# Loading the first weight block of a gated mixer from two DMA queues

## The chip, the core and the metric

The kernel runs on one core of a Trainium2 chip. The metric is the device time in microseconds (us) of one execution; the time before is the median of three runs. The profile comes from one further, profiled execution.

## The reference

The inputs are bfloat16: x is 2048 x 1024. Two branches are computed from the same x and blended per row.

```python
x = A_x
g = _sigmoid((x * gate_w).sum(-1, keepdims=True))
a = _A_ref(x, A_wqkv, A_wo)                 # 32 heads, window of 8 keys at distance 2, softmax, output projection
b = _B_ref(x, B_w_in, B_w_sp, B_b_sp, B_w_out)
return g * a + (1 - g) * b

def _B_ref(x, w_in, w_sp, b_sp, w_out):     # F = 3584, Fh = 1792
    z = _gelu(jnp.einsum('bsd,df->bsf', x, w_in))
    z1 = z[..., :Fh].copy()
    z2 = _layernorm(z[..., Fh:], axis=-1)
    g = jnp.einsum('ts,bsf->btf', w_sp, z2) + b_sp[None, :, None]
    return jnp.einsum('bsf,fd->bsd', z1 * g, w_out)
```

The part that this case is about is the very first product: x times the columns of w_in that give z2.

## The kernel before

Nearly all of SBUF that the kernel uses is one tile, `arena`, cut into regions by hand. `xT` holds x transposed (eight k tiles of 128 rows, 2048 columns). `w2` holds the z2 half of w_in, also as eight k tiles. The instruction order on every engine is the order of the program text (`manual_schedule`); semaphores are added by the framework, and a DMA that reuses a semaphore waits for that semaphore's earlier transfer.

The stages, all paced by TensorE: a warm-up on constants (L91, `warm_up`); the transposes of the first two row tiles (L246) and the `quad`, which is row tiles 0 and 1 times two 512-column blocks of `w2` (both in `z2_quad`); `z2_tile(i, 0)` for row tiles 2 to 15 (L231); q, k and v (L446); the rest of z2 (L231 again); z1 (L482); the spatial product (L496); the output projections and the blend (L509, L519, L527). The attention itself runs on VectorE beside the matmuls, placed by a planner that counts TensorE columns (`Beat`); none of its steps lie in the first 40 us.

What the start consists of:

- SP's queue, in order: row tiles 0 and 1 of x as plain loads into `xn` (L404, 256 KB each); the eight k tiles of w_in's first 1024 z2 columns into `w2` (L406, 256 KB each, 128 rows of 2 KB); then row tiles 2 to 15 of x as transposing loads straight into `xT` (L411), with the first q, k and v weights in between.
- TensorE: seven warm-up matmuls, then 16 transposes of `xn` (L246) into PSUM tiles `pt`.
- VectorE (L250) and ScalarE (L252) each copy half of every `pt` into `xT`: VectorE the k tiles 0, 1 and 4, 5, ScalarE the k tiles 2, 3 and 6, 7, in the order row tile 0 then row tile 1.
- TensorE then runs the quad, k tile by k tile:

```python
for kt in range(KT):
    for i in range(2):
        for c in range(2):
            z2_mm(quad[i][c], i, c, kt, ZW[c])      # L231
```

Each k tile of `w2` is thus read by four matmuls before the next one is needed. After the quad, ScalarE evicts it with Gelu (L236), for which it loads another table first. `z2_tile(2, 0)` is the first to need a row tile that came by a transposing load.

Of the kernel before, what the change touches and what calls it, by code (L numbers as in the profile page):

```python
# [25 lines left out]
FH = 1792  # L26
NF = FH // P
ZC = 512
# [23 lines left out]
def kernel(  # L52
# [13 lines left out]
    nc = tc.nc  # L66
# [10 lines left out]
    def reg(off, n):  # L77
        return arena[:, off:off + n]
# [7 lines left out]
    ones = nc.const_aps.tensor(1.0, [P, 512], BF)  # L86
# [48 lines left out]
    w2 = reg(CD_OFF, KT * W2P).rearrange("p (k c) -> p k c", k=KT)  # L135
# [18 lines left out]
    win_v = B_w_in.rearrange("(k p) c -> p k c", p=P)  # L154
    wsp_v = B_w_sp.rearrange("(a t) s -> a t s", t=P)
    wo_v = A_wo.rearrange("(g h d) n -> g h d n", g=NG, h=HG, d=DH)
    sync = nc.sync
# [244 lines left out]

    for i in range(2):
        sync.dma_start(xn[:, i, :], x_v[:, i, :])  # L404
    for kt in range(KT):
        sync.dma_start(w2[:, kt, 0:2 * ZC], win_v[:, kt, FH:FH + 2 * ZC])  # L406
    for i in range(2, 16):
        if i == 14:
            load_w(0, 2)
# [190 lines left out]
```

## Time and profile before

| | |
|---|---|
| median of 3 runs | 716.31 us (715.63 to 717.37) |
| profiled execution | 715.24 us |
| its span, first to last instruction | 713.5 us |
| TensorE busy | 709.5 us, 99% of the span |
| VectorE, ScalarE, GpSimd busy | 413.7, 246.3, 14.0 us |
| DMA queues with transfers of the kernel | one (q1), 92.36 MB |
| SP's issues L404 / L406 / first L411 | from 0.74 / 1.65 / 5.64 us |
| ScalarE's first table load / first copy L252 | 0.73 / 4.39 us |
| first matmul L231 | 5.67 us |

Times inside the profile count from the first instruction. "SPq" marks an instruction in SP's queue, which issues a DMA; the transfer's landing is given separately, as the time from issue until the last byte is confirmed. "x8" is the number of merged instructions, and a bracket gives the idle time ahead of the first one and what ended it. A matmul is pipelined, so its listed duration is longer than the distance to the next one.

### The profile page before, as it was taken

What the parts mean: (1) busy time and instruction counts of PE and PEld (TensorE: products, weight loads), DVE (VectorE), ACT (ScalarE), POOL (GpSimd) and SP (SyncE); (2) the same over time, 40 slices, a digit from 0 to 9 for tenths busy, and PEclk for the clock granted to TensorE, in tenths of its full rate; (3) what the DMA queues carried; (4) which work ended last, traced back from release to release, by engine and by line L of the source; (5) the groups of instructions that cost most, each with busy time, mean ns of one, the idle gap of its engine ahead of it and who ended that gap; (6) DMA issues with size and microseconds to landing.
All of it is one profiled execution on the core that took longest, in us unless ns stands there. A gap on an engine that the chain in (4) does not pass through costs nothing.

```text
span 713.5 us, 8376 instructions
## 1 busy us (share of the span) xinstructions
PE 709.5 (99%) x3373; PEld 365.1 (51%) x3373; DVE 413.7 (58%) x428; ACT 246.3 (35%) x451; POOL 14.0 (2%) x23
## 2 busy tenths in 40 slices
PE   9999999999999999999999999999999999999998
PEld 4466666666655554444444444444444444444444
DVE  0000589999999999999999999511222112221111
ACT  4434544435379885253331221111111111121111
POOL 1000000000000211000000000000000000000000
PEclk9999999999999999999999999999999999999999
DMA  8974984785673035974449770592400213002210
GB/s 238 191 179 104 255 201 100 202 197 164 176 200 125 0 115 114 208 262 144 173 152 277 275 174 2 184 180 64 132 1 0 54 49 119 1 1 59 60 45 30
DMA packets 176759, 92.89 MB, mean 130 GB/s; under 512 B 145232, under 2 KB 166992, under 8 KB 176208
## 3 DMA queue, kind: packets, MB, share of 16 engines
q1 hardware_dynamic: 176720, 92.36, 48.7%
q8 instruction: 26, 0.43, 0.3%
q14 instruction: 13, 0.11, 0.1%
HBM read 47.71 MB, written 28.38 MB: 107 GB/s over the span
## 4 chain that ended last, share of the span: by engine, by line
PE 99%; DVE 0%; issue 0%; DVEq 0%
PE ps L496 27%; PE ps L446 23%; PE ps L231 14%; PE psb L519 14%; PE ps L482 14%; PE psa L509 8%; PE pw L91 0%; PE pt L246 0%; DVE arena L527 0%; DVE arena L250 0%; DVEq L527 0%
## 5 line engine op out<-in xcount | busy, mean ns | idle before, releaser
L496 PE MATMUL ps<-arena 128*128 128x512 bf16 x896 | 193.9, 379 | 0.0
L446 PE MATMUL ps<-arena 128*128 128x512 bf16 x768 | 165.9, 379 | 0.0
L496 PEld LDWEIGHTS <-arena 128*128 128x128 bf16 x896 | 87.7, 98 | 105.7
L446 PEld LDWEIGHTS <-arena 128*128 128x128 bf16 x768 | 110.7, 144 | 55.1
L519 PE MATMUL psb<-arena 128*128 128x512 bf16 (+2 forms) x462 | 101.6, 373 | 0.0
L274 DVE TENSOR_TENSOR arena<-arena 128x8192 bf16<-128x8192 bf16 x16 | 70.8, 4423 | 51.8 <-DMA arena<-k_d 51.6
L231 PE MATMUL ps<-arena 128*128 128x512 bf16 (+1 forms) x512 | 97.3, 352 | 0.4 <-DVE arena L250 0.4
L527 DVE SCALAR_TENSOR_TENSOR arena<-psb,omg,arena 128x512 bf16<-128x512 f32 (+2 forms) x33 | 24.3, 735 | 125.3 <-PE psb L519 109.3
L482 PE MATMUL ps<-arena 128*128 128x512 bf16 x448 | 96.9, 379 | 0.0
L500 ACT CAST arena<-ps 128x512 bf16<-128x512 f32 x56 | 32.8, 586 | 162.4 <-PE ps L496 135.7
L449 ACT CAST arena<-ps 128x512 bf16<-128x512 f32 x96 | 55.7, 585 | 92.8 <-PE ps L446 88.2
L277 DVE TENSOR_TENSOR arena<-arena 128x4096 bf16<-128x4096 bf16 (+1 forms) x64 | 77.5, 1210 | 1.9
L231 PEld LDWEIGHTS <-arena 128*128 128x128 bf16 x512 | 50.1, 98 | 47.3 <-issue 0.5
L519 PEld LDWEIGHTS <-arena 128*128 128x128 bf16 x462 | 44.7, 98 | 52.1
L307 DVE TENSOR_TENSOR arena<-arena,att_A 128x8192 bf16<-128x8192 bf16 x16 | 70.7, 4422 | 0.2
L482 PEld LDWEIGHTS <-arena 128*128 128x128 bf16 x448 | 43.9, 98 | 52.6
L501 DVE TENSOR_TENSOR arena<-arena 128x512 bf16<-128x512 bf16 x56 | 23.6, 422 | 72.3 <-ACT arena L500 72.3
L526 ACT ACTIVATE arena<-psa,g_s 128x512 f32<-128x512 f32 (+2 forms) x33 | 22.2, 674 | 122.9 <-PE psa L509 109.7
L509 PE MATMUL psa<-arena 128*128 128x512 bf16 (+2 forms) x264 | 60.0, 373 | 0.0
L484 ACT ACTIVATE arena<-ps 128x512 bf16<-128x512 f32 x56 | 32.2, 597 | 52.4 <-PE ps L482 39.4
L236 ACT ACTIVATE arena<-ps 128x512 bf16<-128x512 f32 (+1 forms) x64 | 34.3, 538 | 24.4 <-PE ps L231 24.3
L509 PEld LDWEIGHTS <-arena 128*128 128x128 bf16 x264 | 25.6, 98 | 30.0
(53 smaller groups left out, 258.4 us busy)
## 6 DMA issues: line engine op xcount, KB each, us to landing
arena<-k_d SPq DMA_DIRECT2D x8, 960.0 KB, 7.5
arena<-v_d SPq DMA_DIRECT2D x8, 960.0 KB, 5.1
z_d<-arena SPq DMA_DIRECT2D x14, 512.0 KB, 3.7
arena<-z_d SPq DMA_DIRECT2D x4, 1792.0 KB, 7.1
arena<-in_A_wqkv_dram SPq DMA_DIRECT2D x24, 256.0 KB, 4.6
arena<-in_B_w_in_dram SPq DMA_DIRECT2D x4, 1024.0 KB, 6.6
q_d<-arena SPq DMA_DIRECT2D x32, 128.0 KB, 2.3
k_d<-arena SPq DMA_DIRECT2D x32, 128.0 KB, 2.3
```

What stands on the lines that cost most here:

```text
L231: nc.tensor.matmul(ps[:, 0:N], xT[:, kt, i * P:(i + 1) * P], w2[:, kt, ZC * c:ZC * c + N], start=(kt == 0), stop=(kt == KT - 1))
L236: nc.scalar.activation(z2[:, i, ZC * c:ZC * c + n], ps[:, 0:n], ACT.Gelu_apprx_tanh, accum_out=s1[:, 4 * i + c:4 * i + c + 1])
L274: TT(prod.rearrange("p (w j c) -> p w j c", w=W, j=8, c=C), in0, in1, ALU.mult)
L277: return lambda: TT(pv[:, :, 0:half], pv[:, :, 0:half], pv[:, :, half:2 * half], ALU.add)
L307: TT(prod.rearrange("p (w j d h) -> p w j d h", w=W, j=8, d=DH, h=HG), in0, in1, ALU.mult)
L446: nc.tensor.matmul(ps[:].rearrange("p (t c) -> p t c", t=4), lhsT, wgt[:, :, kt, :], start=(kt == 0), stop=(kt == KT - 1))
L449: nc.scalar.copy(st[:, j % 4, :], ps[:])
L482: nc.tensor.matmul(ps[:], w1[:, kt, (f % 4) * P:(f % 4 + 1) * P], xT[:, kt, 512 * c:512 * (c + 1)], start=(kt == 0), stop=(kt == KT - 1))
L496: nc.tensor.matmul(ps[:], z2[:, i, f * P:(f + 1) * P], wsp[:, i, :, :].rearrange("p a t -> p (a t)"), start=(i == 0), stop=(i == 15))
L500: nc.scalar.copy(gsb, ps[:])
L509: nc.tensor.matmul(psa[:, 0:nw], oT_slots[a % 3][:, kt, :], wo_sb[:, kt, n0:n0 + nw], start=(kt == 0), stop=(kt == KT - 1))
L519: nc.tensor.matmul(psb[:, 0:nw], z1c[:, f, aa * P:(aa + 1) * P], w_out_sb[:, f, n0:n0 + nw], start=(f == 0), stop=(f == NF - 1))
```

## The change

ScalarE first copies 16 columns of the constant ones into the place where k tile 0 of `w2` is going to land. K tiles 0, 2, 4 and 6 are then loaded by DMAs that ScalarE issues, and k tiles 1, 3, 5 and 7 by SP, behind x's two row tiles as before. The load of k tile 0 overwrites the 16 columns, so it waits for the copy, and the three loads behind it on ScalarE wait with it.

```diff
     for i in range(2):
         sync.dma_start(xn[:, i, :], x_v[:, i, :])
+    nc.scalar.copy(w2[:, 0, 0:16], ones[:, 0:16])
     for kt in range(KT):
-        sync.dma_start(w2[:, kt, 0:2 * ZC], win_v[:, kt, FH:FH + 2 * ZC])
+        queue = sync if kt % 2 else nc.scalar
+        queue.dma_start(w2[:, kt, 0:2 * ZC], win_v[:, kt, FH:FH + 2 * ZC])
     for i in range(2, 16):
```

In the changed program the order on ScalarE is: table load, the new copy, the loads of k tiles 0, 2, 4 and 6, the four copies L252, the Gelu table load. The fourth of these loads waits for x's row tile 1, whose semaphore it reuses. On SP it is: row tiles 0 and 1, k tiles 1, 3, 5 and 7, row tile 2 and so on; row tile 2 waits for k tile 1, whose semaphore it reuses (before: k tile 0's). On TensorE nothing is added, removed or reordered.

## The prediction

> **What bounds the kernel now.** I read the page's first part, then the chain of waits over the first 13 us, the timeline of the same stretch, and last the DMA view in windows narrow enough to hold one transfer each.
>
> ```profile
> PE 709.5 (99%) x3373; PEld 365.1 (51%) x3373; DVE 413.7 (58%) x428; ACT 246.3 (35%) x451; POOL 14.0 (2%) x23
> ```
>
> TensorE is busy for 709.5 of 713.5 us. Whatever happens to loads in the first 15 us is therefore worth what it moves TensorE's stream by, and no more. The chain shows where that stream is not closed:
>
> ```profile
> 0.77 2.82 PE pw L91 x7
> 3.60 1.71 PE pt L246 x16
> 5.31 0.02 issue
> 5.33 0.30 DVE arena L250
> 5.64 0.03 issue
> 5.67 7.50 PE ps L231 x34
> ```
>
> Warm-up matmuls and the 16 transposes run until 5.31, and the first real matmul (L231, k tile 0 of the quad) starts at 5.67: a gap of 0.36 us. The chain names the VectorE copy L250, which is the fourth one, as the releaser. That copy writes k tiles 4 and 5 of row tile 1, which the first matmul does not read. The DMA view gives the transfer that it does read:
>
> ```profile
> arena<-in_A_x_dram SPq DMA_DIRECT2D x1, 256.0 KB, 2.4
> ...
> arena<-in_B_w_in_dram SPq DMA_DIRECT2D x1, 256.0 KB, 4.0
> ...
> arena<-in_B_w_in_dram SPq DMA_DIRECT2D x1, 256.0 KB, 4.2
> ...
> arena<-in_B_w_in_dram SPq DMA_DIRECT2D x1, 256.0 KB, 4.4
> ...
> arena<-in_A_x_dram SPq DMA_TRANSPOSE x1, 5.8
> ```
>
> These are x's row tile 0 (issued at 0.74), then k tiles 0, 1 and 2 of w_in (issued at 1.65, 2.12 and 2.60), then row tile 2 (issued at 5.64). The last column is the time from issue to landing. So k tile 0 lands at 1.65 + 4.0 = 5.65, which is what the first matmul waited for; k tile 1 at 6.32, k tile 2 at 7.00. The same view gives 7.57, 8.24, 9.12, 9.80 and 10.41 for k tiles 3 to 7, and 4.09 for row tile 1. The timeline has the queues:
>
> ```profile
> 0.73 1.28 ACT L252 ACT_TABLE_LOAD   x1 [0.73 <-PEq L584]
> 0.74 0.87 SPq L404 DMA_DIRECT2D arena<-in_A_x_dram  x2
> ...
> 1.65 3.89 SPq L406 DMA_DIRECT2D arena<-in_B_w_in_dram  x8
> ...
> 4.39 1.65 ACT L252 COPY arena<-pt 128x256 bf16<-128x256 bf16 x4 [2.37 <-DVE arena L250]
> ...
> 5.64 8.78 SPq L411 DMA_TRANSPOSE arena<-in_A_x_dram  x5
> 5.67 8.58 PE L231 MATMUL ps<-arena 128*128 128x512 bf16 x39 [0.37 <-DVE arena L250]
> ```
>
> SP issues a transfer every 0.47 us, but k tiles land 0.57 to 0.88 us apart: the transfers, not the issues, set the pace (the DMA engines' share is 0.97 and more from 3.6 us on). L231 matmuls follow each other every 0.217 us (112 in 24.33 us by the chain over 30 us), so the quad reads a new k tile every 0.87 us and finishes in 6.94 us. Each later k tile has more to spare than the one before: k tile 1 is needed at 6.54, k tile 7 at 11.76. Only k tile 0 is late.
>
> **The change, part by part.** *The hold.* ScalarE now copies 128x16 values first. Its table load stays at 0.73 and ends at 2.01. A copy can follow a table load directly:
>
> ```profile
> 203.36 1.28 ACT L236 ACT_TABLE_LOAD   x1
> 204.66 0.60 ACT L236 ACTIVATE arena<-ps 128x512 bf16<-128x512 f32 x1
> ```
>
> A 128x16 instruction of ScalarE takes 0.21 us (L387, 208 ns), and the step from a finished copy to what waits for it is about 0.03 us (L250's first copy ends at 4.35, L252 starts at 4.39). So k tile 0 is issued at 2.01 + 0.01 + 0.21 + 0.04 = 2.27 instead of 1.65, 0.62 us later. ScalarE has nothing else until 4.39, so the copy itself costs nothing; without that idle time it would cost its 0.21.
>
> *Where k tile 0 lands.* No transfer in this trace comes from ScalarE's queue, so I bound it. From below: with nothing ahead of it, as for row tile 0, it lands 2.4 us after issue, at 4.67, earlier than now. From above: if the DMA engines serve it only after all four odd tiles, it takes k tile 4's present landing, 8.24. Between these: SP's queue goes from x straight to k tile 1, issued at 1.65 and next to move when x is through. K tiles 0 and 1 are then in flight together, and 512 KB take as long side by side as in turn. Both end where the second ends today, at 6.32. I take 6.32, because it needs only that bytes move at the rate the landings show and that two queues share them evenly.
>
> *The first matmul.* Now its weight load is done (4.995 to 5.14) before k tile 0 lands, and only the matmul waits, 0.02 us. In the changed program the weight load carries the wait for k tile 0, so it follows the landing; L246's loads and their matmuls start 0.11 us apart. First matmul: 6.32 + 0.02 + 0.11 = 6.45, against 5.67: **+0.78 us**. Bounds: below, 5.21, when the third L250 copy ends that the quad's third matmul reads (-0.46); above, 8.24 + 0.13 = 8.37 (+2.70).
>
> *The other k tiles.* All eight still move the same 2 MB. With a start at 6.45, k tile 1 is needed at 7.32, 2 at 8.19, 7 at 12.5; even if each pair lands with its later member, the landings above are 7.57 for 2 and 3, 9.12 for 4 and 5, 10.41 for 6 and 7. Cost 0. If this cover were gone, each late tile would cost its lateness.
>
> *ScalarE's queue.* Four issues at 0.47 us (SP's price) from 2.27, the last also waiting for row tile 1's landing (4.09) by the reuse of its semaphore: done by about 4.6. Behind them stand the four L252 copies, which start at 4.39 now: 0.2 us later. Their first reader is k tile 2's weight load, at 7.18 now and 7.96 then. At twice the price per issue the copies would still have started by 6.1, and the third, which row tile 1's weights need at 8.4, would end by 7.4. Cost 0 either way. Behind the copies the Gelu table load (6.05) has until 12.12.
>
> *SP's queue.* Four issues fewer, so SP is free at 3.65 instead of 5.54. But row tile 2 reuses a semaphore: now it waits for k tile 0 (issued 5.64, the landing was 5.65), in the changed program for k tile 1. At 6.32 + 0.03 + 5.8 it lands at 12.15; the quad's end, where it is needed, moves to 6.45 + 6.94 = 13.39. Cost 0, gain 0: row tiles landing sooner release nothing, since no L231 wait behind the quad shows in the waits of TensorE from 12 to 200 us.
>
> *The sum.* 0.78 us, all of it ahead of a stream that is closed to its end. The profiled execution is 715.24 (span 713.5 and 1.7 around it): 716.02. The three timed runs have a median of 716.31, 1.07 above the profiled one, from 715.63 to 717.37. On the median: **717.1 us**. Of this kernel a measurement tells about 0.2%, 1.43 us, from no change; the forecast lies within it.
>
> **Rivals.**
>
> *K tile 0 keeps its place (no change, or a little gain).* If an engine turns to the other queue after each whole transfer, then with x's last rows running when k tile 0 arrives, k tile 0 is next, ahead of k tile 1, and lands near 5.65 as now: +0.11, 716.4. In a run where no slow engine holds it up, it could land nearer 5.1, and the bound is -0.46: 715.85. For it: in the DMA view data begin to move about 1.0 us after the first issue, so at 2.27 + 1.0 k tile 0 would meet x's tail, which lands at 4.09. Against: nothing here shows turns. The Trainium skill's DMA: Bandwidth & Descriptors (Queues, rings and completion order) says that each engine goes round its queues and drains a packet of some 9 to 17 descriptors from one before it turns to the next, about one of these transfers' share on an engine; by that rule the time would be this rival's. The trace has one queue only and cannot show it.
>
> *K tile 0 stands behind the odd tiles (slower).* SP's are issued at 1.65, 2.12, 2.60 and 3.07, with two ahead of 2.27. If engines take work in order of issue, k tile 0 is third and lands at k tile 2's 7.00: first matmul at 7.13, +1.46, 717.8. If they empty SP's queue first, it is fifth: +2.70, 719.0. The point that decides is a landing past 6.97. For it: the DMA engines are full from 3.6 us on, and a k tile lands 4.0 to 5.3 us after its issue where row tile 0 took 2.4, so there is a line to stand in. Against: a queue of its own need not wait behind another's.
>
> *TensorE's clock falls back in the longer gap (slower).* The warm-up's weight loads are 0.43 us apart, L231's 0.217: half speed until some 5.2, 4.4 us after the first matmul. The gap in TensorE grows from 0.36 to 1.14 us. If that were enough to lose full speed and it took 4.4 us to regain, 2.2 us of work would be lost on top: +2.98, 719.3. Against: the 0.36 us gap did no harm. The Trainium skill's TensorE: Matmul & The Clock Gate (What's actually happening) has the clock fall only after an idle window of about 3.4 us; by that rule 1.14 us cost no speed, and the trace agrees as far as its 0.36 us go.
>
> **How the numbers follow.** Forecast (+0.78) 0.42; place kept 0.15; behind the odd tiles 0.27; clock 0.11; something that gains over 1.43 us 0.05, for which I see no mechanism: the whole gap is 0.36 us and the copies allow 0.46. Within 0.2%: 0.42 + 0.15 = 0.57. Slower: 0.27 + 0.11 = 0.38. Faster: 0.05. The range runs from the gain's bound, 715.85, less 0.4 for the scatter of a median of such runs, to the clock rival: 715.4 to 719.3. For the likeliest case alone: 716.3 to 717.9.
>
> **What would show it.** In the changed profile: ScalarE's copy near 2.0 and its four DMA issues from 2.27; the first L231 matmul near 6.45, released by w_in's transfer; then L231 closed at 0.217 us spacing, and the end as much later as the first matmul. A start at or before 5.8 means place kept; past 7.1, behind the odd tiles; a start near 6.45 with spacing 0.43 after it, the clock. A gap in L231 behind the quad would mean that row tiles or ScalarE's copies became late, which I put at nothing.

## Result: 0.5% slower; in the trace, half of it a late first tile, half of it a slow clock

The changed kernel takes 719.58 us (median of 7 runs, 717.23 to 720.83), the kernel before 715.80 (7 runs, 715.52 to 717.37) beside it: ratio 1.0047, 95% interval 1.003 to 1.0063. A second comparison (last experiment) gave 1.006 (1.0045 to 1.0075). The profiled execution has a span of 716.9 us against 713.5, so 3.4 us are to be found. (The medians differ by 3.8; the traces account for the profiled executions.)

The page of the changed kernel: busy times, the two DMA queues, the chain by engine.

```profile
PE 711.3 (99%) x3373; PEld 365.3 (51%) x3373; DVE 413.7 (58%) x428; ACT 246.7 (34%) x452; POOL 14.0 (2%) x23
...
q1 hardware_dynamic: 176144, 91.31, 48.2%
q10 hardware_dynamic: 576, 1.05, 0.4%
...
PE 99%; DMA 1%; ACT 0%; DVE 0%; issue 0%; DVEq 0%
```

TensorE has the same 3373 matmuls and is busy 1.8 us longer: some of its work ran slower. And 1% of the chain is now a DMA. The chain over the first 13 us says where:

```profile
0.73 1.28 ACT L405
2.01 0.01 issue
2.02 0.21 ACT arena L405
2.24 0.02 issue
2.26 4.99 DMA arena<-in_B_w_in_dram
7.25 0.14 issue
7.38 5.73 PE ps L231 x18
```

The hold is as costed: table load, copy, issue at 2.26. But k tile 0 lands at 7.25, and the first L231 matmul starts at 7.38 instead of 5.67: 1.71 us. The other half stands in the windows of the same profile (columns: stretch, its length, busy time of PE, PEld, DVE, ACT and POOL, granted clock, DMA share, GB/s):

```profile
5.20:7.30 2.10, 0.18 (x3) 0.00 (x0) 0.45 (x2) 2.03 (x4) 0.00 (x0) 1.00 1.01 348
7.40:8.59 1.19, 1.19 (x6) 0.56 (x7) 0.00 (x0) 0.02 (x1) 0.00 (x0) 1.00 1.04 382
8.60:12.00 3.40, 3.40 (x10) 1.21 (x8) 0.00 (x0) 0.00 (x0) 0.00 (x0) 0.50 1.19 258
12.01:15.40 3.39, 3.39 (x17) 1.54 (x16) 0.00 (x0) 0.00 (x0) 0.00 (x0) 1.00 0.87 197
```

TensorE does nothing for 2 us, works 1.2 us at full speed, and then has half its clock for 3.41 us (8.59 to 12.01): 8 weight loads where the next stretch has 16. At 0.427 us per matmul instead of 0.216 that stretch loses 3.41 x 0.495 = 1.69 us. 1.71 + 1.69 = 3.40, the whole difference.

Where k tile 0 spent its 5 us, by the DMA view. First the time to landing of SP's k tile 1 (issued 1.64), SP's k tile 3 (2.12) and ScalarE's k tile 0 (2.26); then what the queues moved in 2.0 to 4.2 us, and in 4.6 to 6.4 (q1 is SP's queue, q10 ScalarE's; packets, MB, share of the 16 engines):

```profile
arena<-in_B_w_in_dram SPq DMA_DIRECT2D x1, 256.0 KB, 5.3
...
arena<-in_B_w_in_dram SPq DMA_DIRECT2D x1, 256.0 KB, 6.1
...
arena<-in_B_w_in_dram ACTq DMA_DIRECT2D x1, 256.0 KB, 5.0
...
q1 hardware_dynamic: 363, 0.67, 85.0%
...
q1 hardware_dynamic: 182, 0.34, 54.8%
q10 hardware_dynamic: 126, 0.24, 41.8%
```

Until past 4.2 only SP's queue moves: x, then k tile 1. ScalarE's queue moves its first data at 4.45, 2.2 us after the issue, and from then on both move, 0.34 and 0.24 MB in the 1.8 us shown. Three tiles are in flight at once, and all three land late: 6.9, 7.25 and 8.2, where the kernel before had landed its first three at 5.65, 6.32 and 7.00.

### The profile page after: what moved, and what is told of

Its sections match the earlier page's. It is cut to its first block, busy times and chain, and to the rows that moved or that the text cites. A ratio compares the mean times of both kernels' runs of the same rounds, so it can differ in the third digit from the quotient of the medians.

```text
span 716.9 us, 8378 instructions
## 1 busy us (share of the span) xinstructions
PE 711.3 (99%) x3373; PEld 365.3 (51%) x3373; DVE 413.7 (58%) x428; ACT 246.7 (34%) x452; POOL 14.0 (2%) x23
## 4 chain that ended last, share of the span: by engine, by line
PE 99%; DMA 1%; ACT 0%; DVE 0%; issue 0%; DVEq 0%
PE ps L498 27%; PE ps L448 23%; PE ps L231 14%; PE psb L521 13%; PE ps L484 13%; PE psa L511 8%; DMA arena<-in_B_w_in_dram 1%; ACT L405 0%; DVE arena L529 0%; ACT arena L405 0%; DVEq L529 0%
## 5 line engine op out<-in xcount | busy, mean ns | idle before, releaser
L231 PE MATMUL ps<-arena 128*128 128x512 bf16 (+1 forms) x512 | 99.0, 356 | 2.0 <-DMA arena<-in_B_w_in_dram 2.0
L231 PEld LDWEIGHTS <-arena 128*128 128x128 bf16 x512 | 50.4, 99 | 50.2 <-issue 4.5
```

What stands on the lines that cost most here:

```text
L231: nc.tensor.matmul(ps[:, 0:N], xT[:, kt, i * P:(i + 1) * P], w2[:, kt, ZC * c:ZC * c + N], start=(kt == 0), stop=(kt == KT - 1))
```

## The experiments

### Filling TensorE's gap

```diff
         quad = [[psum.tile(...) for c in range(2)] for i in range(2)]
+        for _ in range(9):
+            nc.tensor.matmul(quad[0][0][:], ones[:, 0:P], ones[:], start=True, stop=True)
```

> The changed kernel, with nine more 128x512 matmuls on constants (their result is overwritten) between the transposes and the quad, so that TensorE works while k tile 0 is on its way. Theory A: of the 3.4 us that the change costs, 1.7 are the later landing of k tile 0 (first L231 matmul at 7.38 instead of 5.67) and 1.7 are a stretch of 3.41 us at half speed that the 2 us gap in TensorE brings about. Then with the gap filled the first L231 matmul stays near 7.4, all L231 matmuls stand 0.217 us apart, and the span is about 715.2. Rival B: the half-speed stretch from 8.6 to 12.0 comes from something else at the start (the second DMA queue, the fuller DMA engines) and stays: span about 716.9, L231 at 0.43 us from 8.6 to 12.0.

Ratio 1.0025 (1.0016 to 1.0035), against 1.0047 (1.003 to 1.0063) without the nine matmuls; the two come from separate comparisons, and their intervals just meet, so the clock is the firmer sign. The stretch that had half the clock, in the windows of this kernel:

```profile
8.60:12.00 3.40, 3.40 (x17) 1.51 (x17) 0.00 (x0) 0.00 (x0) 0.00 (x0) 1.00 1.15 205
```

Full clock, though in this execution k tile 0 landed later still (first L231 matmul 8.31, not 7.4: row tile 1 came at 5.46, k tile 0 at 8.18), so the span is 716.1 and not the expected 715.2. None of its 10 executions has a mean clock under 0.999; five of the changed kernel's seven have 0.998 or 0.995. Theory A holds: the gap brings the slow stretch.

### One queue, k tile 0 second, third, fifth

```diff
-    for kt in range(KT):
+    for kt in (1, 0, 3, 2, 5, 4, 7, 6):      # second; third: (1, 3, 0, 5, 2, 7, 4, 6); fifth: (1, 3, 5, 7, 0, 2, 4, 6)
         sync.dma_start(w2[:, kt, 0:2 * ZC], ...)
```

> The kernel before, all from SP's queue, with neighbouring k tiles swapped (1, 0, 3, 2, 5, 4, 7, 6), so that k tile 0 moves second, in the place that the prediction gave it. Theory of the place: k tile 0 lands near 6.3, first L231 matmul at 6.35 (+0.7), span 714.2, and the gap of 1.0 us in TensorE leaves the clock alone. Rival on the clock: a gap of 1.0 us is already enough for a stretch of 3.41 us at half speed: span 715.9. Rival on the place: the landing depends on stragglers among the DMA engines and not on the place: first L231 matmul within 0.2 of 5.67, span 713.5.

> The kernel before, all from SP's queue, with the k tiles in the order 1, 3, 0, 5, 2, 7, 4, 6: k tile 0 moves third, with one queue and no copy. Theory: what the change costs is the length of TensorE's gap, whichever queue makes it. In third place k tile 0 lands at 7.0 to 7.4, first L231 matmul 7.0 to 7.4, a gap near the changed kernel's 2.0 us; so the span is 713.5 + 1.5 = 715.0 in the executions that keep the clock and 716.7 in those with a half-speed stretch of 3.41 us, and some show the stretch. Rival: the half-speed stretch needs the second queue (the one-queue gap of 1.4 us of the kernel with k tile 0 second did not bring it): then no execution shows it and the time is +1.5 us, ratio 1.002.

> One queue again, k tiles in the order 1, 3, 5, 7, 0, 2, 4, 6: k tile 0 moves fifth, first L231 matmul at 8.3 to 8.8 (+2.9), a gap of 3.2 us or more in TensorE. Theory of the gap: most executions lose the clock for one stretch of 3.41 us (+1.7) or for two: span 716.4 + 1.7 = 718.1 or 719.8, ratio near 1.006. Rival (the clock depends on the second queue and not on the gap): full speed throughout, span 716.4, ratio 1.004.

Second: ratio 1.0010 (0.9999 to 1.0021). The chain:

```profile
2.11 4.55 DMA arena<-in_B_w_in_dram
...
6.71 5.77 PE ps L231 x26
```

The first L231 matmul is 1.04 us late in the trace (0.7 was expected); the clock is full there, and the mean clock is 1.000 in all ten executions. Third: 1.0027 (1.0016 to 1.0038), half clock from 8.50 to 11.91 in the trace, mean clock 0.998 in two of seven executions. Its chain:

```profile
2.59 4.63 DMA arena<-in_B_w_in_dram
...
7.27 5.95 PE ps L231 x19
```

K tile 0 lands at 7.22, where the changed kernel had 7.25: in these two traces a place behind two other tiles in one queue costs as much as the second queue does. Fifth: 1.0069 (1.0052 to 1.0086), first L231 matmul at 8.41, mean clock 0.998 in three of four executions. So the gap alone does it, with one queue and no copy, and the rivals that needed the second queue fall. The fifth-place trace itself shows a form that was not expected: the clock does not fall, it rises for the first time only at 12.97.

### No hold

```diff
-    nc.scalar.copy(w2[:, 0, 0:16], ones[:, 0:16])
```

> The changed kernel without the small copy: ScalarE issues k tiles 0, 2, 4 and 6 from 0.73 on, beside x's row tiles. It tells why k tile 0's first data moved only at 4.4, 2.2 us after its issue. Theory of the line (what is already in line on the DMA engines goes first): with nothing in line the first data of ScalarE's queue move 1.0 to 1.4 us after issue, as SP's do, and then share with x: row tile 0 lands at 3.8 to 4.2 instead of 3.5, row tile 1 at 5 or later, the transposes end past 6, first L231 matmul 6.3 to 6.8, span 714.2 to 714.7, unless the gaps cost clock (+1.7). Rival (a late start that belongs to ScalarE's queue): first data of that queue 2.2 us after issue here too, at 2.9; x keeps its landings 3.5 and 4.3, k tile 0 lands near 5, first L231 matmul near 5.3, span 713.2.

Ratio 1.0021 (1.001 to 1.0032). ScalarE's queue moves its first data 1.2 us after issue (0.73 to 1.9), beside x, whose row tiles land at 4.59 (later than expected) and 5.63; first L231 matmul 6.50. ScalarE's queue has no late start of its own: the 2.2 us in the changed kernel are time spent behind what is in line. The theory of the line holds. Here too the clock rose late, at 9.90.

### Which queue has which tile

K tile 0 back on SP (the copy then goes into k tile 2's place); only k tile 0 on ScalarE; and k tile 1 held as well, so that k tile 0 is in line first:

```diff
-        queue = sync if kt % 2 else nc.scalar
+        queue = sync if kt % 2 or kt == 0 else nc.scalar      # first
+        queue = sync if kt else nc.scalar                     # second
         queue.dma_start(...)
+        if kt == 0:                                           # third, with the changed kernel's queues
+            nc.scalar.copy(w2[:, 1, 0:16], ones[:, 0:16])
```

> The changed kernel with k tile 0 back on SP, right behind x; ScalarE issues only k tiles 2, 4 and 6, held by the same copy (into k tile 2's place). Theory: the loss hangs on k tile 0's queue alone. K tile 0 lands near 5.65, first L231 matmul 5.7 to 5.8; k tile 1 then shares with k tile 2 and lands at 6.5 to 7, needed at 6.6, so at most 0.4 us of stall follow; no half-speed stretch; span 713.5 to 714.1. Rival: two queues at once hold up every tile behind x (slower engines, stragglers): first L231 matmul past 6.3 although k tile 0 is first in line, span 714.2 or more, with the clock stretch 715.9.

> The changed kernel with only k tile 0 on ScalarE's queue, held as before; k tiles 1 to 7 on SP. Theory: k tile 0 arrives behind k tile 1 in the line and then shares the engines with k tiles 1, 2 and 3, row by row; which tiles stand behind it does not matter. First data of ScalarE's queue at 4.1 to 4.5, first L231 matmul 6.9 to 7.5, span 714.7 to 715.3, or 1.7 more where the gap costs the clock. Rival: the cost comes from the four tiles in each queue, that is from the even tiles that compete with the odd ones: with one tile k tile 0 lands near 6.3 and the span is 714.3 with full clock.

> The changed kernel, with a second small copy, into k tile 1's place, behind ScalarE's issue of k tile 0: now k tile 1, and all of SP's tiles behind it, are issued later than k tile 0. Theory (work that is already in line on the DMA engines goes first, then the two queues share): k tile 0 is in line directly behind x, its first data move by 3.7 instead of 4.45, it shares only once k tile 1 arrives near 4, and it lands near 5.5 to 6.2; first L231 matmul 5.6 to 6.3, span 713.4 to 714.1, no half-speed stretch. Rival (SP's queue is preferred, or ScalarE's starts 2 us after issue in any company): first data of ScalarE's queue not before 4.2, k tile 0 past 6.5, span 714.4 or more.

K tile 0 on SP: ratio 1.0022 (1.0005 to 1.0038), a miss. In the trace 14 of the 16 engines had delivered k tile 0 by 5.2, the last at 7.53, and the clock fell. The spans of its eight executions go from 713.6 to 717.2, so both sides of the expectation occurred. Why one engine took so long is not shown.

Only k tile 0 on ScalarE: 1.0049 (1.0034 to 1.0064), as much as the whole change, with a mean clock of 0.998 in all four executions. SP's k tile 2 (issued 2.12) and ScalarE's k tile 0 (2.26), by the DMA view, and the slow stretch:

```profile
arena<-in_B_w_in_dram SPq DMA_DIRECT2D x1, 256.0 KB, 5.3
...
arena<-in_B_w_in_dram ACTq DMA_DIRECT2D x1, 256.0 KB, 5.4
```

```profile
8.79:12.19 3.40, 3.40 (x10) 1.22 (x8) 0.00 (x0) 0.00 (x0) 0.00 (x0) 0.50 1.21 288
```

The two end together, at 7.42 and 7.64, a little later than expected (first L231 matmul 7.78, not 6.9 to 7.5). One tile on the other queue is enough, if it is the first one needed.

K tile 1 held too: 1.0030 (1.0013 to 1.0048). The DMA view of k tile 0 (issued 2.26) and k tile 1 (2.92), and the waits of TensorE from 5 to 20 us (total, times, longest):

```profile
arena<-in_B_w_in_dram ACTq DMA_DIRECT2D x1, 256.0 KB, 3.2
...
arena<-in_B_w_in_dram SPq DMA_DIRECT2D x1, 256.0 KB, 4.7
```

```profile
PEld L231 <- DMA arena<-in_B_w_in_dram: 1.5, 1, 1.5
PE ps L231 <- DMA arena<-in_B_w_in_dram: 1.0, 1, 1.0
```

The theory of the line holds for k tile 0: issued at 2.26 as in the changed kernel, but in line before k tile 1, it lands at 5.51 and the first L231 matmul starts at 5.64. The expected span does not hold: now k tile 1 lands at 7.61, 1.1 us after it is needed (fifteen of the 16 engines had delivered it by 6.82), and the stall has only moved one tile on. This trace is one of the two shortest of seven executions (spans 714.4 to 719.1, two with a mean clock below 1.000), so its 1.1 us do not account for the median's 2.4.

### One queue, but ScalarE's

```diff
-        queue = sync if kt % 2 else nc.scalar
+        queue = nc.scalar
         queue.dma_start(...)
+    nc.gpsimd.tensor_copy(xT[:, 0, 2 * P:2 * P + 16], w2[:, 0, 0:16])
```

> All eight k tiles from ScalarE's queue, in order, held by the same copy, and none from SP; a 128x16 copy on GpSimd from the landed k tile 0 into row tile 2's place keeps SP's row tiles behind k tile 0, as a semaphore does in the kernel before. The late issue of k tile 0 (2.26) is as in the changed kernel, but nothing shares the engines with it. Theory (the loss is the sharing of two queues, not the hold): k tile 0 goes directly behind x, first data near 3.5, landing 4.9 to 5.6, first L231 matmul 5.2 to 5.7, span 713.1 to 713.7, ratio 0.9995 to 1.0005; ScalarE's L252 copies start near 6.1 and are still early enough. Rival (the late issue itself, or ScalarE's queue, is slow): first L231 matmul 6.3 or later, span 714.2 or more.

Ratio 1.0007 (0.9997 to 1.0016), just above the range expected. The hold and ScalarE's queue cost 0.5 us by this ratio, with an interval from nothing to 1.1 us, so most of the change's loss goes when no tile of SP's stands in front of k tile 0 or beside it; that the late issue costs nothing is not shown. The profiled execution is one of the two longest of ten (spans 715.7 and 715.8, the others 713.5 to 714.3), and by itself it meets the rival's terms: one DMA engine delivered k tile 0 late (15 of 16 by 5.5, the last at 6.29), and the chain and the weight loads show the late rise of the clock again:

```profile
2.26 4.03 DMA arena<-in_B_w_in_dram
...
6.42 6.64 PE ps L231 x23
```

```profile
8.94 0.15 PEld L231 LDWEIGHTS <-arena 128*128 128x128 bf16 x1 [0.28 <-issue]
9.36 0.15 PEld L231 LDWEIGHTS <-arena 128*128 128x128 bf16 x1 [0.28 <-issue]
9.66 1.39 PEld L231 LDWEIGHTS <-arena 128*128 128x128 bf16 x7 [0.15 <-issue]
```

Loads 0.43 us apart until 9.5, seven in 1.39 us after it; yet the page's mean clock is 1.00, because the trace's clock records begin with the first rise.

### Filling the gap where the clock always fell, and the change again

The nine matmuls of the first experiment in the kernel that has only k tile 0 on ScalarE's queue; and the changed kernel unaltered, beside it.

> The kernel with only k tile 0 on ScalarE's queue (all four of its executions lost 3.41 us to half speed), with nine matmuls on constants between the transposes and the quad, whose result is overwritten. Theory of the gap: no execution has a half-speed stretch behind the quad's start; the landing of k tile 0 is unchanged (7.2 to 7.8), so the ratio falls from 1.0049 to 1.0025 or so, the span from 717.1 to 715.4. Rival (the clock falls for another reason than TensorE's idleness): ratio stays at 1.0045 to 1.005.

> The changed kernel once more, beside the other two on the same chip. Theory: ratio 1.004 to 1.006; most executions with one half-speed stretch of 3.41 us (mean clock 0.998), k tile 0 landing at 7.0 to 7.8. Rival (the first comparison had an unlucky share of such executions): ratio 1.002 to 1.003, most with full clock.

With the gap filled 1.0031 (1.0019 to 1.0043) instead of 1.0049 (1.0034 to 1.0064), again from separate comparisons whose intervals overlap. The mean clock is 1.000 in six of six executions, where it was 0.998 in four of four (five of the six have the trace's span, 716.0), and the trace has no half-speed stretch from 6.68 on. Its chain shows the filling matmuls end where k tile 0 lands:

```profile
5.42 2.63 PE ps L255 x9
...
8.18 4.91 PE ps L231 x22
```

The change again: 1.0060 (1.0045 to 1.0075); in its trace k tile 0 landed at 7.75 and the half-speed stretch runs from 8.06 to 11.47. That most executions would show a mean clock of 0.998 did not come true: the other three have 1.000, and spans of 718.0 to 718.5. A late rise would give that, but there is no trace of them to show it.

### One sum for all thirteen traces

The table is about the profiled executions, one of each kernel. Lateness is that of the L231 stream against 5.67 (with k tile 1 held, its stall at k tile 1); the slow time is how long L231 matmuls ran at half speed, by the clock records, times 0.495.

| kernel | late us | slow us | 713.47 + both | span |
|---|---|---|---|---|
| changed | 1.71 | 1.69 | 716.87 | 716.86 |
| changed, gap filled | 2.64 | 0 | 716.11 | 716.11 |
| one queue, second | 1.04 | 0 | 714.51 | 714.50 |
| one queue, third | 1.60 | 1.69 | 716.76 | 716.74 |
| one queue, fifth | 2.74 | 2.26 (late rise) | 718.47 | 718.44 |
| no hold | 0.83 | 1.68 (late rise) | 715.98 | 715.99 |
| k tile 0 on SP | 1.90 | 1.69 | 717.06 | 717.05 |
| only k tile 0 on ScalarE | 2.11 | 1.69 | 717.27 | 717.26 |
| same, gap filled | 2.51 | 0 | 715.98 | 715.96 |
| k tile 1 held too | 1.13 | 0 | 714.60 | 714.60 |
| all on ScalarE | 0.75 | 1.54 (late rise) | 715.76 | 715.73 |
| changed, again | 2.22 | 1.69 | 717.38 | 717.38 |

The kernel before is the thirteenth, at 0 and 0. No trace needs a third term.

## Why the prediction was right and wrong

- **What bounds the kernel**: right. TensorE's stream is closed behind the quad's start, and every us of lateness reached the end (table). That k tile 0 was the late one, and not the L250 copy that the chain named, was right too.
- **The hold, ScalarE's queue, SP's queue, the other k tiles**: right at nothing. The copy ran from 2.02 to 2.23, the issues from 2.26; L252 started at 4.66; no wait at L231 follows the quad's start in the changed profile.
- **Where k tile 0 lands**: this step failed first. It took 6.32 and +0.78 us, the place of the second transfer in one line, because k tile 0 would share the engines with k tile 1 alone. The price of that place was about right: with one queue and k tile 0 second, the ratio of 1.0010 is 0.7 us (interval from nothing to 1.5) where the sum said 0.78. What was wrong is the place. Two of SP's tiles were issued ahead of it (1.64 and 2.12, against 2.26); k tile 0's data began only at 4.45, behind k tile 1, and then shared the engines with k tile 3, so that it landed at 7.25 and cost 1.71 us. The prediction's upper bound, 8.24, held it. The rival "behind the odd tiles" was the nearer one: third in order of issue, +1.46 by its sum, +1.71 measured, and 7.22 for the landing with one queue and k tile 0 third.
- **"K tile 0 keeps its place"**: refuted by the changed kernel's landing. The rule of the Trainium skill's DMA: Bandwidth & Descriptors (Queues, rings and completion order) that stood beside it, a whole packet from one queue before the next, would by an estimate let one of two tiles end a transfer's time ahead (about 0.66 us, the distance of two landings in one queue). The traces are divided on it. With only k tile 0 on ScalarE the two tiles ended 0.22 us apart, and in the changed kernel's first trace both queues moved alike from 4.9 to 5.5 (44 packets from ScalarE's, 45 from SP's); in its second trace ScalarE's moved 81 there and SP's 26, after 11 and 88 in the 0.6 us before, which looks like turns. K tile 0 did not come next either way, because k tile 1 was in line before it.
- **The clock rival**: right in kind, and priced at 2.2 us, measured 1.69: the clock fell not at the quad's start but 1.2 us into it, and came back after 3.41 us and not 4.4. With the landing that the prediction named the clock would most likely have held, as it did through 1.5 us of idle time with k tile 0 second. What failed is that the clock was tied to the forecast's gap, as a case with 0.11, and not to the longer gap of the tile behind the odd ones, so that the two costs were never added. The Trainium skill's TensorE: Matmul & The Clock Gate (What's actually happening) lets the clock fall after an idle window of about 3.4 us; the slow stretches here are 3.41 us long, which agrees with the window's length, but 2.0 us without a matmul were enough, and there the measurement decides.
- **The numbers**: 717.1 was named, "within 0.2%" was given the most; the median of 719.58 is 0.47% slower and stands just above the range's end of 719.3. Two rivals came true together, and no case of the prediction held their sum. That the end of the range came so near is luck: it was 0.78 + 2.2, and the trace has 1.71 + 1.69.

## What to carry to other kernels

Where transfers set the pace and not their issue, moving half of a line to a second queue doesn't shorten it: what was in line before goes first or shares, and the tile needed first pays. Have the tile that a waiting engine needs first issued before its neighbours; a queue of its own does not do that (only k tile 0 on ScalarE cost as much as the whole change). When a change can lengthen a gap in TensorE's work near its start, price the gap twice, once as lateness and once as clock, and if the gap can't be closed, matmuls on constants in it can win the second price back, as in the two kernels with a filled gap.

## What the runs showed of the hardware

- Every fall of the clock ahead of the kernel's end, in five traces, is one stretch of 3.41 us at half speed, starting 3.41 us after the first rise. An idle time of 1.5 us within those 3.41 (one queue, second) left the clock; 2.0 us (third; changed) could take it. With k tile 0 third the mean clock says that it did so in two executions of seven; that the gap's place against these stretches decides it, beside its length, is a reading and not shown. Two executions of the changed kernel have 0.995, twice the loss of one such stretch; no trace of them exists.
- The other form is a late first rise: at 4.4 to 5.4 us in nine traces and at 6.7 in one with the gap filled, but at 9.5, 9.9 and 13.0 in three with idle time before it. Counted back from those rises in steps of 3.41 us, TensorE was idle for 0.8 us or more in each stretch that could have ended in an earlier rise (behind the warm-up), and at most 0.3 us in the one that did. A mean clock of 1.00 does not exclude it; the spacing of weight loads, 0.43 or 0.22 us, does.
- The kernel before shows a mean clock of 0.998 in 2 of the 54 executions beside the experiments, so it is not wholly safe either; no trace tells whether its short gap did it.
- In every trace some single rows of 2 KB take 0.4 us or more (up to 1.4) instead of 0.08, with one queue too, and one to four of the 16 engines often land 0.8 us and more after the others; with k tile 0 on SP beside ScalarE's queue the last was 2.3 us behind the fourteenth. In the changed kernel's second trace fifteen engines had delivered k tile 0 by 6.70 and the last at 7.75, so part of that lateness is one engine's. What makes these rows slow, and whether they alone put an engine behind, stays open.
